# From the third chunk on the first FFN product by Strassen's scheme, with attention pieces at fixed places

## The chip, the cores and the metric

The kernel runs on one core of one Trainium2 chip. The metric is the device time of one execution in microseconds; lower is better. Five engines work side by side, each through its own queue in order: TensorE (PE in the profile; its weight loads are PEld) multiplies, VectorE (DVE) and ScalarE (ACT) do elementwise work and read what TensorE has left in PSUM, GpSimd (POOL) does elementwise work in SBUF, and SyncE (SP) issues the transfers. An instruction that needs another engine's result waits for a semaphore, and everything behind it on its engine waits with it.

## The reference

```python
k_p = k.reshape(B, H, Sp, pool, D).mean(axis=3)      # B = H = 8, S = 576, D = 64, pool = 8, Sp = 72
v_p = v.reshape(B, H, Sp, pool, D).mean(axis=3)
scores = scale * np.matmul(q, k_p.transpose(0, 1, 3, 2))
attn = np.exp(scores - np.max(scores, axis=-1, keepdims=True))
attn = attn / (np.sum(attn, axis=-1, keepdims=True) + 1e-09)
attn_out = np.matmul(attn, v_p)
x = attn_out.transpose(0, 2, 1, 3).reshape(B * S, H * D)      # 4608 tokens x 512
h = x @ w_in                                                  # 512 x 2048
g = np.maximum(h, 0.0) + alpha * np.minimum(h, 0.0)
return (g @ w_out).astype(np.float32)                         # 2048 x 512
```

Keys and values are pooled by eight, each query attends to 72 pooled keys, and the result goes through a feed-forward network (FFN) with a PReLU between its two products.

## The kernel before, in words

The 4608 tokens are cut into nine chunks of 512 (NC = 9, CH = 512). Chunk c has an attention, a first FFN product (w_in, PReLU) and a second one (w_out). A batch entry has 576 tokens, so a chunk spans one or two entries, and all chunks but 0 and 8 bring in one new entry whose K and V are loaded and pooled.

**Precision.** Every fp32 (or wider) operand is split into a high and a low fp16 part, and each product is three matmuls: low by high, high by low, high by high, all added up in PSUM. A weight block of 128x128 is the stationary side.

**FFN.** `ffn1_products(c, f)` (L763) makes the 128 features of block f (16 blocks) for 512 tokens: 4 blocks of K, three matmuls each, 12 matmuls of 512 columns into one PSUM bank of `ps_h`. `ffn1_scaled` (L776, ScalarE), `ffn1_prelu` (L780, VectorE) and `ffn1_parts` (L788 high part on ScalarE, L791 low part on GpSimd) turn it into `g`. `ffn2(c, i)` (L821) makes 128 tokens by 512 outputs: 16 blocks, three matmuls of 512 columns each (L817 to L819), an eviction (L807) and a store (L812). So a chunk has 192 matmuls of 512 columns in each FFN product. The very last tile is made in two halves of 256 columns.

**Attention of a chunk**, per 128-token tile i of four: scores (L602 to L604, 144 columns), maximum L511, subtraction L525, exponential L528 (ScalarE), sum L530, reciprocal L534, scaling L536 (GpSimd), the fp16 parts in `apad` (L545, L548, L551), and a DMA that transposes them into `aT` (L556). Before that K is loaded (`kraw`) and pooled (L376), q is loaded (`qraw`), its maximum taken (L382), the maxima are spread over the partitions (L206 on ScalarE, L209 on TensorE, then L212, L217, L233, L238 on VectorE), and K and q are split (L426, L429, L442, L446). V is loaded (`vraw`), pooled on GpSimd (L467) and split. At the end `mix` (L606, matmuls L613) multiplies by V, and L570 and L574 write x in two fp16 parts.

**Order.** Chunk 0, with the preparation of the weights and the attention of chunks 0 and 1, is ordered by a planner with costs and ranks (`_Plan`, `start`, under a manual schedule). From chunk 1 on the main loop (L924 to L942) writes the code of a chunk, and the attention of the next chunk is dealt out evenly in small groups of operations behind each feature block f, tied by `issue_after` to the last transposition, x and store; the mixes follow the second tile of the second product. A scheduler then orders each engine's queue by its own estimate of when operands are ready, so first and second products, scores and mixes of a chunk stand interleaved on TensorE.

**Buffers.** `big` has 12 buffers of 8 KB per partition; eight of them hold the fp16 weights once they are converted, and kraw, qraw and vraw take turns in the others. `fp` has 4 buffers (pooled K and V, the PReLU tiles, output tiles), `wp` 3 for the exponentials. PSUM: `ps_s` (2 tiles of two banks), `ps_h` and `ps_o` (2 banks each).

## Time and profile before

| what | value |
|---|---|
| runs of the kernel | 872.87, 871.46, 872.85 us; median 872.85 |
| profiled execution: span from the first to the last instruction | 870.4 us (no time of its own besides) |
| granted TensorE clock, mean | 0.994 |
| PE / DVE / ACT / POOL busy | 836.8 / 426.2 / 413.7 / 371.1 us |
| one second product's matmuls plus one first product's | 384 per chunk |
| HBM read / written | 45.10 / 9.44 MB |

Busy times of TensorE come from modelled ends: a matmul's own duration (379 ns for 512 columns) is longer than the step from one to the next, so what a matmul costs is read from the starts in the timeline. A row of a timeline gives start, duration, engine, line, operation, out<-in, shape, count, and in brackets the idle time ahead of it with what ended it. A row of the groups gives the count, then busy time and mean duration, then the idle time ahead with its releasers. SPq rows are SyncE's issues of transfers, not the transfers.

### The profile page before, as it was taken

What the parts mean: (1) busy time and instruction counts of PE and PEld (TensorE: products, weight loads), DVE (VectorE), ACT (ScalarE), POOL (GpSimd) and SP (SyncE); (2) the same over time, 40 slices, a digit from 0 to 9 for tenths busy, and PEclk for the clock granted to TensorE, in tenths of its full rate; (3) what the DMA queues carried; (4) which work ended last, traced back from release to release, by engine and by line L of the source; (5) the groups of instructions that cost most, each with busy time, mean ns of one, the idle gap of its engine ahead of it and who ended that gap; (6) DMA issues with size and microseconds to landing.
All of it is one profiled execution on the core that took longest, in us unless ns stands there. A gap on an engine that the chain in (4) does not pass through costs nothing.

```text
span 870.4 us, 11545 instructions
## 1 busy us (share of the span) xinstructions
PE 836.8 (96%) x4452; PEld 409.4 (47%) x4452; DVE 426.2 (49%) x657; ACT 413.7 (48%) x700; POOL 371.1 (43%) x375
## 2 busy tenths in 40 slices
PE   5769899999999999999999999999999999999998
PEld 4444344445444444454445444544454454444445
DVE  3989998377228621772177207820881156112210
ACT  4989985455425541554145325632562255213330
POOL 1257456187316830683067406731573047203320
PEclk9989999999999999999999999999999999999999
DMA  9686234513710471037003701371126005100000
GB/s 332 229 254 242 78 79 73 180 31 73 209 51 6 83 197 32 20 73 209 26 27 72 210 25 27 66 202 40 28 53 144 17 20 94 37 24 13 1 25 25
DMA packets 122902, 78.87 MB, mean 91 GB/s; under 512 B 106176, under 2 KB 107008, under 8 KB 122848
## 3 DMA queue, kind: packets, MB, share of 16 engines
q1 hardware_dynamic: 122848, 78.14, 33.1%
q8 instruction: 35, 0.57, 0.3%
q14 instruction: 19, 0.16, 0.1%
HBM read 45.10 MB, written 9.44 MB: 63 GB/s over the span
## 4 chain that ended last, share of the span: by engine, by line
PE 85%; DVE 6%; ACT 4%; DMA 3%; issue 1%; SPq 1%; ACTq 0%; DVEq 0%
PE o L817 13%; PE o L819 13%; PE o L818 13%; PE h L770 12%; PE h L771 12%; PE h L772 12%; PE x L613 2%; DMA qraw<-qT_dram 1%; DMA nat<-kN_dram 1%; PE s L602 1%; PE s L603 1%; PE s L604 1%; DVE t L780 1%; PE h L817 1%; PE h L818 1%
## 5 line engine op out<-in xcount | busy, mean ns | idle before, releaser
L791 POOL TENSOR_TENSOR g<-t,g 128x512 f16<-128x512 f32 x144 | 171.9, 1195 | 329.0 <-ACT g L788 327.8
L780 DVE SCALAR_TENSOR_TENSOR t<-t,al 128x512 f32<-128x512 f32 x128 | 128.7, 1007 | 269.1 <-ACT t L776 259.8
L770 PE MATMUL h<-x,w 128*128 128x512 f16 x576 | 218.3, 379 | 4.7 <-DVE w2e L233 1.9
L771 PE MATMUL h<-x,w 128*128 128x512 f16 x576 | 218.3, 379 | 1.1 <-DVE x L574 1.0
L772 PE MATMUL h<-x,w 128*128 128x512 f16 x576 | 218.3, 379 | 0.0
L817 PE MATMUL o<-w,g 128*128 128x512 f16 (+1 forms) x560 | 208.1, 373 | 2.5 <-POOL g L791 1.7
L818 PE MATMUL o<-w,g 128*128 128x512 f16 (+1 forms) x560 | 208.8, 373 | 0.0
L819 PE MATMUL o<-w,g 128*128 128x512 f16 (+1 forms) x560 | 205.6, 373 | 0.0
L788 ACT CAST g<-t 128x512 f16<-128x512 f32 x144 | 88.6, 615 | 115.0 <-DVE t L780 114.5
L776 ACT ACTIVATE t<-h,rp 128x512 f32<-128x512 f32 x144 | 97.9, 681 | 59.6 <-PE h L772 58.9
L807 ACT ACTIVATE o<-o,os 128x512 f32<-128x512 f32 x33 | 22.5, 688 | 165.6 <-PE o L819 165.6
L817 PEld LDWEIGHTS <-g 128*128 128x128 f16 x592 | 57.9, 98 | 69.0 <-POOL g L791 2.7
L467 POOL TENSOR_TENSOR vraw<-vraw 72x512 f32<-72x512 f32 (+1 forms) x56 | 56.6, 1028 | 77.8 <-DMA vraw<-vT_dram 66.8
L819 PEld LDWEIGHTS <-g 128*128 128x128 f16 x592 | 57.9, 98 | 66.5
L771 PEld LDWEIGHTS <-w 128*128 128x128 f16 x576 | 56.3, 98 | 69.0 <-issue 7.1
L818 PEld LDWEIGHTS <-g 128*128 128x128 f16 x592 | 57.9, 98 | 65.5 <-issue 1.3
L772 PEld LDWEIGHTS <-w 128*128 128x128 f16 x576 | 56.3, 98 | 68.7 <-issue 1.6
L770 PEld LDWEIGHTS <-w 128*128 128x128 f16 x576 | 56.3, 98 | 65.0 <-issue 0.6
L574 DVE SCALAR_TENSOR_TENSOR x<-x,xsc,x 128x512 f16<-128x512 f32 x36 | 25.9, 747 | 73.2 <-ACT x L570 73.2
L536 POOL TENSOR_TENSOR e<-e,sm 128x576 f32<-128x576 f32 x35 | 46.2, 1321 | 12.6 <-DVE sm L534 12.2
L548 POOL TENSOR_TENSOR apad<-e,apad 128x448 f16<-128x448 f32 x36 | 40.8, 1134 | 16.0 <-ACT apad L545 16.0
L545 ACT CAST apad<-e 128x576 f16<-128x576 f32 x44 | 28.9, 670 | 24.9 <-POOL e L536 13.9
(137 smaller groups left out, 843.5 us busy)
## 6 DMA issues: line engine op xcount, KB each, us to landing
w<-w_dram SPq DMA_DIRECT2D x16, 1024.0 KB
out_dram<-o SPq DMA_DIRECT2D x35, 256.0 KB
qraw<-qT_dram SPq DMA_DIRECT2D x17, 512.0 KB
vraw<-vT_dram SPq DMA_DIRECT2D x28, 288.0 KB
kraw<-kT_dram SPq DMA_DIRECT2D x12, 576.0 KB
apad<-apad SPq DMA_DIRECT2D x28, 144.0 KB
kq<-kT_dram SPq DMA_DIRECT2D x2, 576.0 KB
nat<-kN_dram SPq DMA_DIRECT2D x2, 512.0 KB
```

What stands on the lines that cost most here:

```text
L467: nc.gpsimd.tensor_tensor(out=o, in0=y, in1=z, op=ALU.add)
L536: x = add("DVE" if i in on_dve else "Pool", us, lambda ex=ex, sm=sm, eng=eng: eng.tensor_tensor(out=ex(), in0=ex(), in1=sm().broadcast_to( ...
L770: nc.tensor.matmul(ps, w[:, 1, ks_], x[:, 0], start=(n == 0), stop=False)
L771: nc.tensor.matmul(ps, w[:, 0, ks_], x[:, 1], start=False, stop=False)
L772: nc.tensor.matmul(ps, w[:, 0, ks_], x[:, 0], start=False, stop=(n == NK - 1))
L776: nc.scalar.activation(t, hps[c, f], AF.Copy, scale=rp[:, f:f + 1])
L780: nc.vector.scalar_tensor_tensor(out=t, in0=t if c else h, scalar=(al if c else ra)[:, f:f + 1], in1=t, op0=ALU.mult, op1=ALU.max)
L788: nc.scalar.copy(out=g[:, 0], in_=t)
L791: nc.gpsimd.tensor_tensor(out=g[:, 1], in0=t, in1=g[:, 0], op=ALU.subtract)
L817: nc.tensor.matmul(ps, g[:, 1, ts_], w[:, 0, cs], start=(f == 0), stop=False)
L818: nc.tensor.matmul(ps, g[:, 0, ts_], w[:, 1, cs], start=False, stop=False)
L819: nc.tensor.matmul(ps, g[:, 0, ts_], w[:, 0, cs], start=False, stop=(f == NF - 1))
```

## The change

From chunk 2 on (`FAST = 2`) the first FFN product is made by the Winograd form of Strassen's scheme, one level deep: features by halves (the even and the odd block of each pair), K by halves and tokens by halves. Seven products of blocks replace eight. For each group d of four feature blocks there are seven `product` calls, each of 12 matmuls (2 pairs q, 2 blocks of K, 3 precision parts) of 256 columns, into three banks x, y and z that are added to more than once:

```diff
+    def product(c, d, bank, n, m, begin, end):
+        if begin:
+            hb[d, bank] = ps_b.tile([P, 2, HC], F32, tag="b", name="h")
+        ps, x = hb[d, bank], xs[c][m]()
+        for q in range(2):
+            for k in range(2):
+                for e, (l, r) in enumerate(((1, 0), (0, 1), (0, 0))):
+                    nc.tensor.matmul(ps[:, q], weights(n, 2 * d + q, l, k), x[:, r, k],
+                                     start=begin and not (q or k or e), stop=end and q + k + e == 4,
+                                     skip_group_check=True)
+    def plus(d, bank, j, n, o=None):
+        z = half(d, j, n)
+        nc.vector.tensor_tensor(out=half(d, *o) if o else z, in0=hb[d, bank], in1=z, op=ALU.add)
+    def fast_begin(c, d):
+        product(c, d, "x", "a11", "b11", True, False)
+        ht[d, 1] = hp_.tile([P, 2, CH], F32, tag="h", name="h1")
+        nc.scalar.copy(out=half(d, 1, 0), in_=hb[d, "x"])
+    def fast_end(c, d):
+        product(c, d, "y", "a22", "t4", False, True)
+        plus(d, "y", 1, 0)
+        product(c, d, "z", "s4", "b22", False, True)
+        plus(d, "z", 0, 1)
+        for j in (1, 0):
+            for q in range(2):
+                f = 4 * d + 2 * q + j
+                hs[c, f] = t = ht[d, j][:, q]
+                nc.scalar.activation(t, t, AF.Copy, scale=rp[:, f:f + 1])
+                nc.vector.scalar_tensor_tensor(out=t, in0=t, scalar=al[:, f:f + 1], in1=t, op0=ALU.mult, op1=ALU.max)
+                ffn1_parts(c, f, 0)
+                ffn1_parts(c, f, 1)
+    def fast_rest(c, d):
+        product(c, d, "y", "s2", "t2", True, False)
+        ht[d, 0] = hp_.tile([P, 2, CH], F32, tag="h", name="h0")
+        plus(d, "y", 1, 0, (0, 1))
+        product(c, d, "z", "s1", "t1", True, False)
+        product(c, d, "x", "a12", "b21", False, True)
+        nc.scalar.copy(out=half(d, 0, 0), in_=hb[d, "x"])
+        product(c, d, "y", "s3", "t3", False, False)
+        plus(d, "y", 1, 0, (1, 1))
+        plus(d, "z", 1, 1)
```

Group d's `fast_begin` is written ahead of `fast_end` of group d - 1 and `fast_rest` of group d. Five `plus` (VectorE) and two copies (ScalarE) per group join the seven products in SBUF tiles h1 and h0. The PReLU part is as before.

The operands: `sums` makes the weight sums s1, s2, s4 (in three `big` buffers that are never given back) and s3 (in place of a block that is no longer used), beside the second product of chunk 1. `blocks` takes the place of L570 and L574 behind the mixes: two evictions of 1024 columns, four differences and seven splits.

```diff
+    def sums(i):
+        a = w16_pair(i)
+        r = hp_.tile([P, 2, CH], F32, tag="h", name="wr")
+        f = hp_.tile([P, 4, HC], F32, tag="h", name="wf")
+        nc.vector.tensor_tensor(out=r, in0=a[:, :, 0], in1=a[:, :, 1], op=ALU.add)
...
+        for n in range(4):
+            nc.scalar.copy(out=outs[n][0], in_=f[:, n])
+            nc.gpsimd.tensor_tensor(out=outs[n][1], in0=f[:, n], in1=outs[n][0], op=ALU.subtract)
+    def blocks(add, c, after, rank):
...
+        for n in range(2):
+            add("PE", 1.1, lambda n=n: mix(c, n, ps[n]()), *after, rank=rank)
+            add("ACT", 1.1, lambda n=n: nc.scalar.activation(f[n](), ps[n](), AF.Copy, scale=xsc), rank=rank)
+        add("DVE", 0.75, lambda: less(srcs["t1"], b[0][1], b[0][0], nc.vector))
+        add("DVE", 0.75, lambda: less(srcs["t2"], b[1][1], srcs["t1"], nc.vector))
+        add("Pool", 1.2, lambda: less(b[0][1], b[1][1], b[0][1], nc.gpsimd))
+        for n, eng in (("b11", nc.vector), ("t2", nc.gpsimd), ("t1", nc.vector), ("b21", nc.vector)):
+            add("ACT", 0.62, lambda n=n: hi(n))
+            add("DVE", 0.75, lambda n=n, eng=eng: lo(n, eng))
+        add("DVE", 0.75, lambda: less(b[1][0], b[1][0], srcs["t2"], nc.vector))
+        for n, eng in (("t3", nc.gpsimd), ("t4", nc.vector), ("b22", nc.gpsimd)):
+            add("ACT", 0.62, lambda n=n: hi(n))
+            add("DVE", 0.75, lambda n=n, eng=eng: lo(n, eng))
```

The attention is cut into eleven stages, and the table `AT` gives each a time within a cycle of 78 us whose first 36.6 are the first product; `on(c, t)` writes the stages of chunks c + 1 and c + 2 that are due. Loads, maxima and scales are now written in the second product of the chunk before last, V and the tiles in the first product of the chunk before, the mix in its second product. The `issue_after` ties go, except around `sums`.

```diff
+AT = dict(load=-19.0, max=-17.0, scale=-10.0, tile0=-4.0, loadv=0.0, v=1.0, tile1=12.0, vscale=20.0, tile2=30.0,
+          tile3=38.0, mix=55.0)
...
+    def on(c, t):
+        for n, at in ((c + 1, t), (c + 2, t - CYCLE)):
+            if n not in lines:
+                lines[n] = _Line(n)
+            lines[n].emit(at)
```

Pools: `ps_h` and `ps_o` become one `ps_b` of four banks, shared by both products. After `start`, `fp` and `wp` are replaced by pools of two buffers each, the second `apad` goes, and `hp_` (four fp32 tiles of 128x1024) and `xq` (three more x tiles) come. The scales `xsc` and `wsc` change by a factor of two each. Chunks 0 and 1 make their products as before.

TensorE's order of chunks 2 to 8 now has the narrow products in groups of 12, with scores, and the first products of the next group, between them; at the end of a first product up to 24 matmuls of the second stand ahead of the last two products of the last group. Of the last 48 matmuls of a second product 27 or 28 stand ahead of the three products that spread the maxima of q and K, and the first scores follow after 22 to 26 narrow matmuls of the next chunk.

SyncE's queue, before: the loads for chunk 5 and the stores of chunk 3 (`aT`: transposition; `kraw`, `qraw`, `vraw`: loads of K, q and V; `out_dram<-o`: stores):

```order
L254 DMA kraw_3943<-kT_dram 128x1152
L254 DMA kraw_3945<-kT_dram 128x1152
L254 DMA qraw_3947<-qT_dram 128x1024 x2
L254 DMA vraw_3950<-vT_dram 72x1024 x2
L812 DMA out_dram<-o_3714 128x512
L812 DMA out_dram<-o_3766 128x512
```

The same place in the changed kernel:

```order
L568 DMA_TRANSPOSE aT_3550<-apad0_96 128x16x128
L948 DMA out_dram<-o_4208 128x512
L259 DMA kraw_4345<-kT_dram 128x1152
L948 DMA out_dram<-o_4324 128x512
L259 DMA qraw_4347<-qT_dram 128x1024 x2
L948 DMA out_dram<-o_4395 128x512
L948 DMA out_dram<-o_4506 128x512
L259 DMA vraw_4524<-vT_dram 72x1024 x2
L259 DMA vraw_4527<-vT_dram 72x1024 x2
```

The two halves of K, q and V went out in a row ahead of the stores; now the second half of K, q and V stand between and behind the stores (the first half, kraw_4343, stands eight rows further up).

VectorE's queue in the first product of chunk 4, before (pt, pr, ev, vs: scale of V; mx, e, sm: softmax of a tile; t: PReLU; os: output scale; v16: low part of V):

```order
L212 TENSOR_REDUCE pt_4106<-pm_4104 128x1
L217 TENSOR_SCALAR pr_4108<-pt_4106 128x1
L233 TENSOR_SCALAR ev5_4110<-pr_4108 128x1
L511 TENSOR_REDUCE mx_4153<-s_4138 128x8
L238 TENSOR_SCALAR vs__4131<-ev5_4110 128x1
L801 TENSOR_TENSOR os_5401<-wsc_120,ev5_4110 64x1
L801 TENSOR_TENSOR os_5456<-wsc_120,ev5_4110 128x1
L525 TENSOR_TENSOR e_4155<-s_4138,mx_4153 128x576
L487 SCALAR_TENSOR_TENSOR v16_4133<-vs_4069,vs__4131,v16_4133 72x512
L780 SCALAR_TENSOR_TENSOR t_4171<-t_4171,al_116 128x512
```

The same place now (h1 is the SBUF sum, h_4659 bank y and h_4674 bank z of the second group; vm: the maximum of the pooled V):

```order
L914 SCALAR_TENSOR_TENSOR h0_4543<-h0_4543,al_116 128x512 x2
L247 TENSOR_REDUCE vm_4803<-vs_4587 72x1
L897 TENSOR_TENSOR h1_4611<-h_4659,h1_4611 128x2x256
L523 TENSOR_REDUCE mx_4727<-s_4714 128x8
L897 TENSOR_TENSOR h1_4611<-h_4674,h1_4611 128x2x256
L537 TENSOR_TENSOR e_4729<-s_4714,mx_4727 128x576
L217 TENSOR_REDUCE pt_4810<-pm_4808 128x1
L222 TENSOR_SCALAR pr_4812<-pt_4810 128x1
L238 TENSOR_SCALAR ev5_4814<-pr_4812 128x1
L243 TENSOR_SCALAR vs__4816<-ev5_4814 128x1
```

The additions of the banks (L897) stand among the steps of V and of the softmax, where before there were PReLUs.

More of the change, by code (lines that the diff above doesn't have):

```diff
@@ L302, in big_tile, with attention @@
         return once(lambda: big.tile(shape, F32, tag="big", name=name))
-    def attention(add, c, bs, rank, begin=False, early=False, k_pool=0, q_cuts=1, on_act=(), on_dve=(), behind=()):
+    def attention(add, c, bs, rank, begin=False, early=False, k_pool=0, q_cuts=1, on_act=(), on_dve=(), behind=(), stage=lambda n: None):
+        stage("load")
         n = len(bs) + 2
@@ L384, in attention @@
             ld, rank=rank + 0.18 * i) for i, (q, (t, ld)) in enumerate(zip(q16s[c], ql))]
+        stage("scale")
         scs = []
@@ L499, in attention @@
         for i in range(TPC):
+            stage(f"tile{i}")
             rk = rank + rks["sm"] + rks["sms"] * i
@@ L561, in attention @@
         xd = []
+        stage("mix")
+        if c >= FAST:
+            blocks(add, c, [*td, *vd], rank)
+            return xd, td
         for hp in range(NPR // 2):
```

143 lines of the change are left out of this document (103 added, 40 removed).

## The prediction

> **What bounds the kernel now.** I read the page first, then the chain of work that ended last, the busy time by stretches, the groups of instructions by shape, and the timelines. The page:
>
> ```profile
> span 870.4 us, 11545 instructions
> PE 836.8 (96%) x4452; PEld 409.4 (47%) x4452; DVE 426.2 (49%) x657; ACT 413.7 (48%) x700; POOL 371.1 (43%) x375
> PE 85%; DVE 6%; ACT 4%; DMA 3%; issue 1%; SPq 1%; ACTq 0%; DVEq 0%
> ```
>
> TensorE is busy 96% of the span and carries 85% of the chain. The stretches (length, then busy time of PE, PEld, DVE, ACT, POOL) show where the rest lies:
>
> ```profile
> 160.00:180.00 20.00, 18.89 (x90) 8.69 (x90) 8.00 (x13) 11.09 (x20) 7.16 (x6) 1.00 0.70 223
> 180.00:200.00 20.00, 18.12 (x109) 9.08 (x108) 18.41 (x30) 11.01 (x17) 15.82 (x18) 1.00 0.02 5
> 231.00:320.00 89.00, 89.00 (x482) 42.71 (x481) 42.51 (x64) 37.92 (x61) 40.78 (x41) 1.00 0.39 97
> 408.00:497.00 89.00, 89.00 (x481) 42.72 (x480) 42.00 (x64) 37.75 (x61) 41.04 (x40) 1.00 0.32 83
> 488.00:508.00 20.00, 20.00 (x117) 9.64 (x116) 2.91 (x4) 7.20 (x13) 3.64 (x4) 1.00 0.54 178
> ```
>
> Chunk 1 begins at about 161 us and loses 1.1 + 1.9 us there; in the later stretches TensorE has no gap, at granted clock 1.00 (the column behind POOL), and the other engines have half their time free. So a microsecond taken from TensorE in chunks 2 to 8 is a microsecond of the kernel, as long as the others keep up. The mixes (attention times V) in the chain mark the period:
>
> ```profile
> 229.04 1.91 PE x L613 x32
> 317.91 1.90 PE x L613 x32
> 406.02 1.90 PE x L613 x32
> ```
>
> The period is 88.1 to 88.9 us. The prices of a matmul come from TensorE's timeline, as first and last start of gapless runs:
>
> ```profile
> 254.63 0.38 PE L772 MATMUL h<-x,w 128*128 128x512 f16 x1
> ...
> 256.57 0.38 PE L772 MATMUL h<-x,w 128*128 128x512 f16 x1
> ...
> 276.65 0.23 PE L602 MATMUL s<-kbd,q 128*128 128x144 f16 x1
> ...
> 277.34 0.23 PE L604 MATMUL s<-kbd,q 128*128 128x144 f16 x1
> ...
> 863.04 0.27 PE L819 MATMUL o<-w,g 128*128 128x256 f16 x1
> ...
> 866.97 0.27 PE L819 MATMUL o<-w,g 128*128 128x256 f16 x1
> ```
>
> Nine steps of 512 columns take 1.94 us (0.2156 each), eleven of 144 columns 0.69 (0.063), 36 of 256 columns 3.93 (0.1092). All load new weights each time; a load is hidden even behind 144 columns.
>
> **The gain.** A first FFN product of a chunk is 192 matmuls of 512 columns, 41.4 us. By seven block products it is 4 x 7 x 12 = 336 of 256 columns, 36.7 us. That is 4.7 us less in each of chunks 2 to 8: 32.9 us, all of it on the path.
>
> The Trainium skill speaks against this: "TensorE: Matmul & The Clock Gate", section "Back-to-back issue gap", gives a stream of load-and-matmul pairs about 81 ns at 128 columns and 131 at 512. By these two figures half the columns keep three quarters of the spacing, and the scheme would lose. The rows above deny it here: 0.1092 is 51% of 0.2156.
>
> **What the change puts on the other engines.** The prices, from the groups of instructions (count | busy us, mean ns of one | idle time before and its releasers):
>
> ```profile
> L780 DVE SCALAR_TENSOR_TENSOR t<-t,al 128x512 f32<-128x512 f32 x128 | 128.7, 1007 | 269.1 <-ACT t L776 259.8 <-issue 5.2 <-POOL apad L551 4.0
> L780 DVE SCALAR_TENSOR_TENSOR t<-h,m,t 128x512 f32<-128x512 f32 x16 | 11.8, 747 | 1.1 <-ACT t L776 1.1
> L776 ACT ACTIVATE t<-h,rp 128x512 f32<-128x512 f32 x144 | 97.9, 681 | 59.6 <-PE h L772 58.9 <-ACT t L776 0.5
> L788 ACT CAST g<-t 128x512 f16<-128x512 f32 x144 | 88.6, 615 | 115.0 <-DVE t L780 114.5
> L791 POOL TENSOR_TENSOR g<-t,g 128x512 f16<-128x512 f32 x144 | 171.9, 1195 | 329.0 <-ACT g L788 327.8 <-PE h L772 1.3
> L511 DVE TENSOR_REDUCE mx<-s 128x8 f32<-128x576 f32 x36 | 26.5, 737 | 5.6 <-PE s L604 5.5
> L382 ACT ACTIVATE q<-qraw 128x1024 f16<-128x1024 f32 x17 | 17.8, 1048 | 7.6 <-DMA qraw<-qT_dram 7.6
> L664 DVE SCALAR_TENSOR_TENSOR vw<-vw,w 128x1024 int32<-128x1024 int32 x14 | 17.1, 1224 | 1.2 <-ACT vw L661 1.2
> L530 DVE TENSOR_REDUCE sm<-e 128x8 f32<-128x576 f32 x32 | 23.9, 748 | 17.2 <-ACT e L528 17.2
> L532 DVE TENSOR_SCALAR sm<-sm 128x8 f32<-128x8 f32 x36 | 11.6, 323 | 0.9 <-ACT e L521 0.4
> L206 ACT ACTIVATE pd<-ident,m 128x128 bf16<-128x128 bf16 x42 | 14.6, 395 | 3.1 <-DVE m L242 2.1 <-PE pm L209 0.8
> L242 DVE TENSOR_REDUCE vm<-vs 72x1 f32<-72x512 f32 x8 | 5.4, 673 | 0.0
> L242 DVE TENSOR_REDUCE m<-ks 128x1 f32<-128x288 f32 x8 | 3.6, 447 | 0.8 <-ACT ks L297 0.8
> ```
>
> *Sums of weights*, once, beside chunk 1's second product: 8 times one 128x1024 (L664's 1.22) and four 128x256 operations (nearest row 0.45) on VectorE, 24 us, less on ScalarE, about the same on GpSimd. 41.4 us of TensorE work hide it, in a stage where VectorE is busy 2.9 of 20 us. Uncovered it would cost up to 24; I take 0.
>
> *Blocks of x*, behind each mix: seven high parts and two evictions on ScalarE (7 x 0.615 + 2 x 1.05 = 6.4 us), seven operations on VectorE (7.0 at 1.007), four on GpSimd (4.8 at 1.195). They stand against 22 us of products that follow: 0. The moved scale factors cost nothing.
>
> *First FFN product.* Per group of four feature blocks VectorE gets five additions that read PSUM (`plus`), ScalarE two copies; a product into a bank must wait until the addition before it has read that bank. The tightest place: after `s3`x`t3` into bank y comes `a22`x`t4` into the same bank, with one or two other products (1.3 to 2.6 us) between. VectorE's order at such a place is quoted with the change.
>
> Behind `vm`, which waits for GpSimd's pooling of V, stand two additions for which TensorE waits; before, only PReLUs stood there. VectorE's sum in the stage: 20 additions at 0.75 (14.9), 16 PReLUs at 1.007 (16.1), four tiles of three softmax passes at 0.74 (8.9) and of two small ones at 0.32 or less (2.2), V 2.5 (its maximum 0.67, its low part like a PReLU, five small ones), q 1.24: 45.8 us, against 36.7 + 3.4 of scores = 40.1 on TensorE. Records overlap a little (the rows below: 0.75 long, the next starts 0.67 later), 70 long ones by 0.08, so 40.3 is the true load: equal to TensorE's, with the last tile's part running into the second product. Waits are then between 0 and 45.8 - 40.1 = 5.7 us per stage, in six stages (chunk 8 has no attention beside it: 31 us).
>
> ```profile
> 432.16 0.75 DVE L780 SCALAR_TENSOR_TENSOR t<-t,al 128x512 f32<-128x512 f32 x1 [19.94 <-ACT t L776]
> 432.83 2.60 DVE L376 TENSOR_REDUCE ks<-kraw 128x144 f32<-128x1152 f32 x2
> ```
>
> I take 0.5 a stage, 3 us, nearest to 40.3. I price `plus` by L780's PSUM form (747). The Trainium skill ("SBUF — State Buffer", "Who interferes with whom") says that a VectorE operation with two SBUF inputs contends with a GpSimd one that reads SBUF, and one with a single SBUF input doesn't; by it 747 holds, and if `plus` took 1007 too the sum would be 51.0. The two rows agree with the page, which no run here tries on `plus` itself.
>
> *Loads.* Three of the 12 `big` buffers go to the weight sums for good and eight hold weights, so one is left for K, q and V: each load waits until the one before is used up. SyncE's queue is quoted with the change. K and q once went out together ahead of the stores; now q waits for the second half of K, and that for the reduction of the first, which VectorE does behind the first block of x. The rows, from the timelines of SyncE, VectorE and ScalarE (idle time and releaser in brackets; chunk 1, and chunk 4 from 442 us on):
>
> ```profile
> 163.19 1.34 SPq L254 DMA_DIRECT2D kraw<-kT_dram  x2
> 164.63 0.94 SPq L254 DMA_DIRECT2D qraw<-qT_dram  x2
> ...
> 167.78 1.35 DVE L376 TENSOR_REDUCE ks<-kraw 128x144 f32<-128x1152 f32 x1 [2.36 <-DMA kraw<-kT_dram]
> ...
> 172.10 1.06 ACT L382 ACTIVATE q<-qraw 128x1024 f16<-128x1024 f32 x1 [1.06 <-DMA qraw<-qT_dram]
> ...
> 174.76 1.06 ACT L382 ACTIVATE q<-qraw 128x1024 f16<-128x1024 f32 x1 [1.01 <-DMA qraw<-qT_dram]
> ...
> 442.68 0.55 DVE L212 TENSOR_REDUCE pt<-pm 128x3 f32<-128x384 f32 x1
> ...
> 448.95 2.48 DVE L446 SCALAR_TENSOR_TENSOR q<-qraw,s,q 128x1024 f16<-128x1024 f32 x2
> ```
>
> From the mix to the first scores: eviction 1.05, subtraction 0.75, reduction 1.35, K load 4.6 (163.19 to 167.78), reduction 1.35, q load 7.5 to 10.1 (164.63 to 172.10 or 174.76), maximum 1.05, its spread over partitions 3 x 0.395 and a product, 2.5 in all, pt to the first half of q 7.5 (442.68 to 450.2, PReLUs between): 26.6 to 29.2 us. In TensorE's order lie 102 wide and 22 narrow products between, 24.4 us. The wait is 2.2 to 4.8 us a chunk; without PReLUs, stores and V in the way it is 0. I take 0.8 in each of six chunks, 5 us, near the low end: this order puts scores, mixes and maxima just behind their operands as the old one did, and TensorE shows no gap in the two long stretches quoted.
>
> *Chunk 1*: the `f` buffers fall from 4 to 2, shared with K and V. While K or V holds one, an f takes 0.68 + 1.01 + 0.62 + 1.20 = 3.5 us instead of 2.6, 0.9 for each of up to eight: 7 us at worst. q is loaded earlier, and the 3 us lost now can go: -3 at best. I take +1.
>
> **The sum.** 870.4 - 32.9 + 3 + 5 + 1 = 846.5 us of span. The profiled execution is known by its span; the three runs lie at 871.46 to 872.87, the median 872.85, 2.4 above it. So 849.
>
> **Rivals.**
> - *No waits at all.* The gapless stretches of before speak for it, engines at 90 to 100% in the first product against it: 870.4 - 32.9 + 2.4 = 840.
> - *The single load buffer is the bound.* At 2.5 us in six chunks, 15 instead of 5: 859; at 4.8 it is 29: 873, no gain. For it: the rows of chunk 1; against: there 1 MB of stores and V stood in the same queue.
> - *VectorE is the bound of the first product* (slower). Place: the additions into banks y and z. Price: 5.7 us in six stages, 34.2 instead of 3: 846.5 + 31.2 + 2.4 = 880. It decides from 44.8 us of VectorE time per stage on, where the 4.7 gained are gone. For it: 45.8 by mean durations, PReLUs of up to 2.7 us; against: the overlap of records, and the last group's additions wait beside second products.
> - *The weight loads set the pace of narrow matmuls* (slower). Place: every product of 256 columns. If a load (98 ns by the row below) no longer hid wholly and each step were that and the shortest one seen, 0.063, it would be 0.161: 336 x 0.161 = 54.1, 12.7 us more in seven chunks instead of 4.7 less: 970. For it: the loads grow from 192 to 336; against: the 36 steps of 0.1092. The two figures of the Trainium skill's page would have it so.
>
> ```profile
> L817 PEld LDWEIGHTS <-g 128*128 128x128 f16 x592 | 57.9, 98 | 69.0 <-POOL g L791 2.7 <-issue 1.5
> ```
>
> **How the numbers follow.** Forecast (843 to 856) 0.59; no waits 0.16; load buffer 0.15 (of which 0.02 at no gain); VectorE 0.09; weight loads 0.01. A measurement here can tell 0.2%, 1.7 us. Faster 0.59 + 0.16 + 0.13 = 0.88; same 0.02; slower 0.10. The range is 839 to 862: no waits, forecast, and most of the load case; left out are the slower ones and the worst loads, 0.15 or so.
>
> **What would show it.** Right: 336 products per chunk stepping at 0.109 us, the period near 85 us, PE gaps short and in front of the scores (released by VectorE's q) and of `a22`x`t4` (released by `plus`). The load case: gaps of over 2 us at the maxima's product or the first scores, with ScalarE's maximum waiting for the q load. The VectorE case: `plus` starting late with no idle time ahead of it, and PE waiting for it in every group. Wrong altogether: a step well above 0.11, or more than 5 us of gaps per chunk.

## The result, and the profile after

The changed kernel takes 897.86 us (median of 4 runs, 897.56 to 899.88), the kernel before 872.86: 1.028 times as long, 95% interval 1.0255 to 1.031. Two executions, one of the run e1 below (2487.6 us) and the profiled one of e5 (983.8 us at a granted clock of 0.82), were far slower than the others of their kernel and are left out of all times. The profiled execution has a span of 895.8 us, 25.4 more than before. The head of its page:

```profile
span 895.8 us, 13939 instructions
PE 820.9 (92%) x5460; PEld 514.4 (57%) x5460; DVE 572.0 (64%) x858; ACT 472.8 (53%) x823; POOL 442.8 (49%) x435
PE 36%; DVE 16%; DMA 10%; POOL 10%; issue 5%; ACT 3%; POOLq 0%; SPq 0%; ACTq 0%; DVEq 0%
```

TensorE carried 85% of the chain that ended last and now carries 36%; VectorE, DMA and GpSimd have taken the rest. TensorE's busy time fell by 15.9 us where 32.9 were forecast, and its idle time grew by 895.8 - 820.9 - (870.4 - 836.8) = 41.3 where 9 were. These two differences, 17.0 and 32.3, are the whole miss of 49.3 us.

Where it happened: the stretches from mix to mix (length, then busy time of PE, PEld, DVE, ACT, POOL, then the granted clock), chunk 1's part, chunk 2, and the next three.

```profile
160.00:240.00 80.00, 69.22 (x343) 31.98 (x343) 46.49 (x76) 35.62 (x60) 43.64 (x45) 0.96 0.28 63
240.00:351.00 111.00, 91.93 (x629) 59.70 (x628) 90.18 (x114) 53.42 (x99) 70.45 (x70) 0.90 0.28 68
351.00:441.00 90.00, 86.39 (x599) 57.73 (x598) 59.09 (x84) 45.78 (x74) 47.06 (x45) 0.95 0.35 79
441.00:532.00 91.00, 86.56 (x633) 57.45 (x633) 55.58 (x86) 45.11 (x74) 47.27 (x44) 1.00 0.36 83
532.00:619.00 87.00, 84.44 (x618) 56.72 (x619) 56.42 (x84) 44.53 (x74) 46.76 (x44) 1.00 0.35 84
```

Before, every period from chunk 2 on was 88 to 89 us, and chunk 1's was 74. Now chunk 2 takes 111 with VectorE busy 90 of them, chunks 3 and 4 about 90, and only then does the period come down to 87, where it stays until chunk 7 (85). The granted clock is below 1.00 in the first three stretches, where before it was 1.00 from chunk 1 on. The longest waits of TensorE from chunk 1 on, from its timeline (idle time and releaser in brackets):

```profile
181.49 0.24 PE L675 MATMUL s<-kbd,q 128*128 128x144 f16 x1 [4.43 <-DVE q L455]
216.10 0.38 PE L847 MATMUL h<-x,w 128*128 128x512 f16 x1 [2.14 <-ACT t L853]
270.50 0.26 PE L214 MATMUL pm<-pd,ones 128*128 128x128 bf16 x1 [6.97 <-ACT pd L211]
301.32 2.94 PE L887 MATMUL h<-x,w 128*128 128x256 f16 x15 [2.84 <-ACT h L902]
310.07 2.72 PE L887 MATMUL h<-x,w 128*128 128x256 f16 x12 [5.82 <-DVE h L897]
351.18 2.99 PE L686 MATMUL x<-aT,v 88*64 88x320 f16 x24 [3.62 <-DMA aT<-apad]
410.00 0.27 PE L887 MATMUL h<-x,w 128*128 128x256 f16 x1 [2.17 <-DVE h L897]
531.93 1.70 PE L686 MATMUL x<-aT,v 88*64 88x192 f16 x27 [2.33 <-DMA aT<-apad]
```

The 6.97 us have a history that VectorE's timeline tells:

```profile
228.18 0.91 DVE L857 SCALAR_TENSOR_TENSOR t<-t,al 128x512 f32<-128x512 f32 x1 [1.77 <-ACT t L853]
229.01 1.21 DVE L642 TENSOR_TENSOR wr<-w 128x1024 f32<-128x1024 f16 x1
...
251.72 1.34 DVE L384 TENSOR_REDUCE ks<-kraw 128x144 f32<-128x1152 f32 x1
...
261.17 1.34 DVE L384 TENSOR_REDUCE ks<-kraw 128x144 f32<-128x1152 f32 x1
...
272.15 0.78 DVE L646 TENSOR_TENSOR wf<-wr,wf 128x256 f32<-128x256 f32 x1
272.85 0.54 DVE L217 TENSOR_REDUCE pt<-pm 128x3 f32<-128x384 f32 x1
```

The weight sums are pinned behind chunk 1's last PReLU, which ends at 229; they last until 273, through the blocks of x and into chunk 2's first product. The first K reduction of chunk 3 stands behind four of the eight sums, the beginning of a fifth and the first operations of the blocks of x until 251.7, the second behind more of both until 261.2, and SyncE's and ScalarE's rows hang on it, because there is one load buffer:

```profile
253.08 0.34 SPq L259 DMA_DIRECT2D kraw<-kT_dram  x1
262.54 0.81 SPq L259 DMA_DIRECT2D qraw<-qT_dram  x2
...
266.14 1.06 ACT L390 ACTIVATE q<-qraw 128x1024 f16<-128x1024 f32 x1 [1.64 <-DMA qraw<-qT_dram]
```

Each load is issued as soon as the reduction before it is over. So the sums, priced at nothing, arrive at TensorE by way of the load chain: the late reductions and the one buffer work together.

### The profile page after: what moved, and what is told of

Same layout as the page of the kernel before. It is cut to its first block, busy times and chain, and to the rows that moved or that the text cites. A ratio compares the mean times of both kernels' runs of the same rounds, so it can differ in the third digit from the quotient of the medians.

```text
span 895.8 us, 13939 instructions
## 1 busy us (share of the span) xinstructions
PE 820.9 (92%) x5460; PEld 514.4 (57%) x5460; DVE 572.0 (64%) x858; ACT 472.8 (53%) x823; POOL 442.8 (49%) x435
## 4 chain that ended last, share of the span: by engine, by line
PE 36%; DVE 16%; DMA 10%; POOL 10%; issue 5%; ACT 3%; POOLq 0%; SPq 0%; ACTq 0%; DVEq 0%
PE h L887 10%; PE o L953 8%; PE o L955 8%; PE o L954 8%; DMA aT<-apad 5%; DMA vraw<-vT_dram 4%; POOL vraw L477 3%; DVE h L914 3%; POOL g L868 3%; DVE h L897 2%; DVE wf L646 2%; POOL e L548 1%; PE x L686 1%; DMA apad<-apad 1%; DVE sm L542 1%
## 5 line engine op out<-in xcount | busy, mean ns | idle before, releaser
L887 PE MATMUL h<-x,w 128*128 128x256 f16 x1344 | 166.2, 277 | 13.6 <-DVE h L897 9.7
L868 POOL TENSOR_TENSOR g<-h,g 128x512 f16<-128x512 f32 x112 | 136.5, 1245 | 82.8 <-ACT g L865 82.8
L897 DVE TENSOR_TENSOR h<-h,h 128x512 f32<-128x512 f32 x140 | 94.3, 683 | 70.7 <-PE h L887 60.5
L887 PE MATMUL h<-x,sw 128*128 128x256 f16 x1008 | 126.1, 276 | 0.1
L914 DVE SCALAR_TENSOR_TENSOR h<-h,al 128x512 f32<-128x512 f32 x112 | 112.3, 1055 | 0.8 <-ACT h L913 0.8
L887 PEld LDWEIGHTS <-sw 128*128 128x128 f16 x1008 | 99.3, 99 | 13.3 <-issue 0.2
L913 ACT ACTIVATE h<-h,rp 128x512 f32<-128x512 f32 x112 | 73.9, 713 | 47.3 <-DVE h L897 46.5
L865 ACT CAST g<-h 128x512 f16<-128x512 f32 x112 | 64.5, 616 | 19.8 <-DVE h L914 19.4
L560 POOL TENSOR_TENSOR apad<-e,apad 128x448 f16<-128x448 f32 x36 | 40.1, 1113 | 37.1 <-ACT apad L557 37.1
L847 PE MATMUL h<-x,w 128*128 128x512 f16 x128 | 49.7, 388 | 5.4 <-ACT t L853 3.9
L868 POOL TENSOR_TENSOR g<-t,g 128x512 f16<-128x512 f32 x32 | 37.6, 1182 | 30.2 <-ACT g L865 30.2
L848 PE MATMUL h<-x,w 128*128 128x512 f16 x128 | 49.6, 388 | 1.1 <-DVE x L590 1.0
```

The costliest lines, as they stand in the source:

```text
L847: nc.tensor.matmul(ps, w[:, 1, ks_], x[:, 0], start=(n == 0), stop=False)
L865: last["h"] = nc.scalar.copy(out=g[:, 0], in_=t)
L868: last["g"] = nc.gpsimd.tensor_tensor(out=g[:, 1], in0=t, in1=g[:, 0], op=ALU.subtract)
L887: nc.tensor.matmul(ps[:, q], weights(n, 2 * d + q, l, k), x[:, r, k], start=begin and not (q or k or e), stop=end and q + k + e == 4, skip ...
L897: nc.vector.tensor_tensor(out=half(d, *o) if o else z, in0=hb[d, bank], in1=z, op=ALU.add)
L913: nc.scalar.activation(t, t, AF.Copy, scale=rp[:, f:f + 1])
```

## The experiments

Times are medians, ratios those to the kernel before, measured beside each run, with their 95% interval. Runs are called by their number.

**e1, e2, e3, e4: one suspect each.**

e1 makes no sums and has

```diff
-FAST = 2
+FAST = NC
...
+            for t in sw:
+                nc.vector.memset(t[:, 0, 0, :4], 1.0)
...
+        if c == NC - 2:
+            for t in sw:
+                nc.vector.tensor_scalar(out=t[:, 0, 0, :4], in0=t[:, 0, 0, :4], scalar1=2.0, scalar2=None, op0=ALU.mult)
```

The two small operations were to hold the three buffers `sw` until the end. They do not: the scheduler puts both into chunk 1, at 170 us, and the loads take the buffers from there on. The rows are those of e2, which has the same lines; e5, e7 and e11 have them too, and show the same:

```profile
170.07 0.17 DVE L1112 TENSOR_SCALAR sw<-sw 128x4 f16<-128x4 f16 x1
170.27 8.51 SPq L259 DMA_DIRECT2D kraw<-kT_dram  x2
```

Both halves of K, q and V of chunk 3 go out by 184 us; K is reduced at 246. So e1, e2, e5, e7 and e11 have four load buffers, as the kernel before has, where their expectations speak of three held ones or a single one.

> No product by Strassen's scheme in any chunk; the fixed places of the attention pieces, the smaller pools and the three buffers held for the weight sums stay as in the changed kernel. Before 872.9, changed 897.9. Theory A (three separate losses: chunk 1's two buffers for f, the weight sums, and VectorE with the late transpositions in chunks 2 to 7): only the first and a part of the last remain, chunk 1 about 10 us longer, late transpositions up to 8: 880 to 890. Rival C (the new places and the load buffer cost most of it, whatever the product): 890 or more. Rival B (VectorE's additions and PReLUs alone): within 4 us of before.

Measured: 910.8 us, 1.043 (1.038 to 1.048), in rival C's range, though without its load buffer. The order and the pools alone, even with the loads' buffers given back, are slower than with Strassen's scheme. TensorE's waits name the cause:

```profile
PE h L847 <- ACT t L853: 20.4, 11, 3.3
```

The evictions into f, which now has two buffers, hold the first product up in chunks 1 to 5. In the changed kernel chunk 1 is the only one of these that isn't done by the scheme. e7 and e11 take this apart.

e2 leaves the sums out, with e1's lines on `sw`:

```diff
-        if n in ("s1", "s2", "s4"):
-            return sw[("s1", "s2", "s4").index(n)][:, i, l, cs]
-        j, h = dict(a11=(0, 0), a12=(0, 1), a22=(1, 1), s3=(1, 0))[n]
+        j, h = dict(a11=(0, 0), a12=(0, 1), a22=(1, 1), s3=(1, 0), s1=(0, 0), s2=(0, 1), s4=(1, 1))[n]
...
-                if c == FAST - 1 and f % 8 == 0:
+                if False:
```

> The sums of weights are left out: the products by Strassen's scheme take blocks of the old weights in their place (the numbers are wrong, the number and size of matmuls is the same), the three buffers stay held. Theory A: chunk 2's period of 111 us falls to about 90, the whole by 15 to 22 us, to 876 to 883. Rival B (the first product is bound by VectorE whatever ran before): chunk 2 keeps most of its loss, 892 or more.

Measured: 859.7 us, 0.985 (0.980 to 0.989), 38.2 us less than the changed kernel: twice what even the first theory gave. The gain isn't in chunk 2 alone. Stretches of e2, from chunk 2's mix on:

```profile
245.00:329.00 84.00, 82.14 (x589) 55.07 (x588) 57.93 (x86) 43.62 (x73) 51.28 (x45) 1.00 0.35 84
329.00:413.00 84.00, 83.81 (x615) 56.29 (x612) 54.16 (x84) 44.21 (x74) 49.50 (x45) 1.00 0.34 87
```

Without the sums, and with four load buffers, the scheme gives what was forecast of it: from chunk 3 on periods of 84 to 85 us, hardly a gap, clock 1.00, with nearly the same VectorE time as in the changed kernel's later chunks (54 to 58 us a chunk). So VectorE's time does not bind by itself. But two things were changed here, since the buffers came free with the sums: how much of the 38.2 us each is worth, and what the single buffer would cost without the sums, no run shows.

e3 gives chunk 1 other f buffers:

```diff
-        hs[c, f] = t = fp.tile([P, CH], F32, tag="f", name="t")
+        hs[c, f] = t = (hp_ if c else fp).tile([P, CH], F32, tag="h" if c else "f", name="t")
```

> Chunk 1's sixteen f tiles come out of the four buffers of the other pool, which nothing uses in that stage; K and V keep the two. Theory A: the period of chunk 1 falls from 84.6 towards the 73.9 of before, 6 to 10 us less: 888 to 892. Rival (the gaps of chunk 1 come from the late q load and from the order, not from the f buffers): 895 or more.

Measured: 882.8 us, 1.010 (1.006 to 1.014): 15.1 less, half again as much as the most that the first theory said. In this run TensorE stands still for 11.4 us ahead of chunk 2's mix (at 240.83), and the profile names nothing that it waited for.

e4 leaves one line out of `fast_end` (L914):

```diff
-                nc.vector.scalar_tensor_tensor(out=t, in0=t, scalar=al[:, f:f + 1], in1=t, op0=ALU.mult, op1=ALU.max)
```

> In chunks 2 to 8 the PReLU is left out (16 VectorE operations of 1.06 us less per chunk; ScalarE and GpSimd take the scaled tile at once). Theory A: the waits for additions and copies in the first products go (about 11 us of gaps with 3 to 5 of half clock behind them), the rest stays: 882 to 888. Rival B (VectorE is the bound of the whole loss): below 877.

Measured: 874.7 us, 1.002 (0.999 to 1.004): 23.2 less, in the range of the rival. VectorE's time does decide here. Since e2 has all PReLUs and hardly a gap, it decides together with the sums and the one buffer, where VectorE is already late.

**e5 and e7: do they add up, and what does the order cost?** e5 is e2 and e3 together; e7 is e1 with the f buffers of e3.

> Both edits at once: chunk 1's f tiles out of the other pool, and the sums of weights left out (blocks of the old weights in their place, wrong numbers, the same matmuls). If the sums and chunk 1's two buffers, with all that they make late, are the whole of the miss, what is left is the forecast's sum without these two: 845 to 851. If VectorE or the single load buffer binds by itself, chunks 2 to 7 stay above 86 us a period and the time above 856.

> The run without any Strassen product again, now with f tiles out of four buffers in every chunk. That run lost 39 us against before, with TensorE waiting for ScalarE's evictions into f twice a chunk. If those two buffers are its loss, 870 to 877; if the fixed places or the one load buffer cost by themselves, 885 or more.

Measured: e5 854.8 us (three executions), 0.979 (0.975 to 0.983), only some 5 less than e2, and between its two ranges. The two edits overlap: without the sums and with four load buffers, chunk 1's buffers for f cost little. e7 888.4 us, 1.018 (1.013 to 1.022): above the range for the first case and inside that of the second; with four load buffers, this leaves the places. The f buffers were 22 us of e1's loss, and some 14 remain. TensorE's waits in e7:

```profile
PE x L686 <- DMA aT<-apad: 11.4, 5, 4.8
```

The mix waits for the last transposition in chunk after chunk: the new places put the last tiles too late.

**e8 and e9: loads in halves, done badly.** The single 8 KB load buffer was to become two halves, but K's last third was written ahead of the reduction of the first third, whose place it takes; one third of K is not used, and the order of the waits is not that of two buffers. (e9 also has e3 and four early sums.)

> The changed kernel with the one buffer for K, q and V loads used as two halves in turn (K in thirds, q and V each in pieces that fill a half); sums and chunk 1 as they were. Load theory (the sums make the loads late once, and a single buffer keeps them late in every later chunk): chunks 1 and 2 as before, the periods of chunks 3 to 7 from 88 on average to 84 or 85, 880 to 886. VectorE theory (its work in the first product makes the later waits): 893 or more.

> The three mended together, with all of the work done: f tiles of chunk 1 out of the other pool, halved load buffer, and four of the eight weight sums moved into chunk 1's first product (behind its 6th, 9th, 12th and 15th feature block), the rest into the first half of its second product. If sums, f buffers and loads are the cause, each chunk loses a microsecond or so of waits: 848 to 858. If the sums still cost where they stand now, 860 to 870.

Measured: 905.2 us (1.036, 1.033 to 1.040) and 899.4 (1.029, 1.026 to 1.033), far above their first ranges. They decide nothing on loads. One row of e8 on ScalarE is worth having, though:

```profile
399.04 1.06 ACT L406 ACTIVATE q<-ld 128x1024 f16<-128x1024 f32 x1 [4.09 <-DMA ld<-qT_dram]
...
400.10 0.76 ACT L556 ACTIVATE e<-e,ds 128x576 f32<-128x576 f32 x1
```

An operand that is 4 us late holds the exponential behind it, VectorE's row sum waits for that, and TensorE then waited 4.57 us for the addition behind the row sum. An attention piece that stands too early in an engine's queue can cost as much as one that stands too late.

**e10 to e13: the loads again, the places, the sums' place.** e10 is the edit that e8 was meant to be: the next load is written behind the reduction that empties its half.

```diff
-            step = NPR * S // 2
+            step = NPR * S // (3 if c >= 3 else 2)
...
+                if c >= 3 and a == 2 * step:
+                    later.append(go)
...
+                    if later:
+                        later.pop(0)()
...
+            ld_[:] = [big.tile([P, 2, 1024], F32, tag="big", name="ld"), 0]
```

> The edit that the run of halved loads was meant to be: the one buffer for K, q and V as two halves in turn (K in thirds), now with each later load written behind the reduction or pooling that empties its half, so that nothing is overwritten. Sums and chunk 1 as in the changed kernel. TensorE's order from chunk 3 on is then nearly that of the run without sums (maxima's products 16 us of work behind the mix, for 20.5). Load theory (the sums make the loads late once, a single buffer keeps them late): periods of chunks 3 to 7 fall from 88 to about 85, 880 to 888. If the loads are not what makes the later waits: 893 or more.

Measured: 881.8 us, 1.010 (1.008 to 1.013), 16.1 less, inside the load theory's range. Its stretches, chunk 2 to chunk 4:

```profile
240.00:344.00 104.00, 90.04 (x618) 58.42 (x617) 77.85 (x114) 52.90 (x98) 69.71 (x70) 0.93 0.30 70
344.00:429.00 85.00, 84.39 (x617) 56.33 (x617) 52.85 (x85) 44.88 (x74) 46.28 (x45) 1.00 0.37 86
429.00:517.00 88.00, 85.22 (x626) 57.00 (x626) 55.47 (x87) 45.30 (x74) 47.14 (x44) 1.00 0.31 79
```

Chunk 3 is free of loss at once. A second buffer lets the loads catch up after the sums; with a single one chunks 3 and 4 still take about 90 us, and VectorE, with little to spare, turns late loads into waits. From chunk 4 on (88 us here) the two kernels are within 3 us of each other in every period.

e11 moves the tiles in e7:

```diff
-AT = dict(... tile1=12.0, vscale=20.0, tile2=30.0, tile3=38.0, mix=55.0)
+AT = dict(... tile1=8.0, vscale=20.0, tile2=20.0, tile3=30.0, mix=55.0)
```

> The run without Strassen and with four f buffers (888 against 874 for before), whose only gaps are five waits of the mix for the last transposition, 1.0 to 4.8 us, 11.4 in all: now the tiles' places are moved up (second to fourth tile at 8, 20 and 30 for 12, 30 and 38), which puts the last scores 5 us of TensorE's work further ahead of the mix. If the fixed places make the transposition late: 874 to 880, the waits gone. If the single padded buffer does it, whatever the place: 885 or more.

Measured: 877.3 us, 1.005 (1.003 to 1.0065), and no wait of a mix for the transposition is left. It was the place and not the single padded buffer (`apad`). What the order then still costs without the scheme, and with four load buffers, is about 4 us; the largest wait left is one of 6.0 us for GpSimd at chunk 1's second product.

e12 is e3 with four of the eight sums in chunk 1's first product and four in the first half of its second:

```diff
                 on(c, HALF * f / NF)
+                if f in {5: 0, 8: 1, 11: 2, 14: 3}:
+                    with tc.issue_after(last["p"].ins), tc.issue_after(last["h"].ins), tc.issue_after(last["g"].ins):
+                        sums({5: 0, 8: 1, 11: 2, 14: 3}[f])
...
-                if c == FAST - 1 and f % 8 == 0:
+                if c == FAST - 1 and (i, f) in {(0, 0): 4, (0, 8): 5, (1, 0): 6, (1, 8): 7}:
...
```

> f tiles of chunk 1 out of the other pool (882.8 alone), and half of the weight sums moved up into chunk 1's first product (behind its 6th, 9th, 12th and 15th feature block), the rest into the first half of the second. If it is their place behind the first product that makes chunk 2 late, 868 to 876; if it is their work on VectorE and GpSimd wherever it stands, 880 or more.

Measured: 876.8 us, 1.005 (1.002 to 1.007): 6.0 less than e3, a little above the first range. The place counts; the run stays 4 us above the kernel before.

e13 has all of these (without e11's places) and the operands of the sums in PSUM:

```diff
-        r = hp_.tile([P, 2, CH], F32, tag="h", name="wr")
+        r = ps_s.tile([P, 2, CH], F32, tag="s", name="wr")
...
-        nc.vector.tensor_tensor(out=r, in0=a[:, :, 0], in1=a[:, :, 1], op=ALU.add)
-        a11, a12, a21, a22 = (r[:, j, n * HC:n * HC + HC] for j in range(2) for n in range(2))
+        nc.vector.tensor_tensor(out=r[:, 0], in0=a[:, 0, 0], in1=a[:, 0, 1], op=ALU.add)
+        nc.vector.tensor_tensor(out=r[:, 1, HC:], in0=a[:, 1, 0, HC:], in1=a[:, 1, 1, HC:], op=ALU.add)
+        nc.vector.tensor_tensor(out=f[:, 3], in0=a[:, 1, 0, :HC], in1=a[:, 1, 1, :HC], op=ALU.add)
+        a11, a12, a21, a22 = r[:, 0, :HC], r[:, 0, HC:], f[:, 3], r[:, 1, HC:]
```

> All of it with the work done in full: f tiles of chunk 1, half of the sums early, two half buffers for the loads, and three of the four blocks of each weight sum held in PSUM, so that three of the four additions read one SBUF operand. By the rows of the changed kernel an addition of the sums takes 0.41 us alone and 0.89 beside GpSimd: VectorE's part falls from 33 us towards 25. If sums, f buffers and loads are the loss: 855 to 865. If the sums cost wherever they stand: 872 or more.

Measured: 872.4 us, 1.000 (0.998 to 1.002): the time of before, on the other theory's side. With sums in chunk 1's first product, where VectorE has other work, the waits go there.

**e14 to e17: contention, and another chunk for the sums.** e14 is the changed kernel with the PSUM edit above and nothing else.

> The changed kernel (897.9) with one edit: of each weight sum, a11, a12 and a22 are held in PSUM instead of SBUF, so that three of its four additions read one SBUF operand. Contention theory: those additions take 0.41 for 0.89 us, VectorE's part falls by about 10 us, GpSimd's subtractions from 1.0 to 0.8, and chunk 2 starts its attention earlier: 885 to 892. If the sums cost by their place alone: 895 or more.

Measured: 884.5 us, 1.013 (1.011 to 1.016), 13.4 less, just below its first range. The groups of the sums' additions and of GpSimd's subtractions behind them, changed kernel:

```profile
L646 DVE TENSOR_TENSOR wf<-wf,wr 128x256 f32<-128x256 f32 x8 | 6.6, 828 | 0.0
L646 DVE TENSOR_TENSOR wf<-wr,wf 128x256 f32<-128x256 f32 x8 | 5.9, 740 | 0.1
L650 POOL TENSOR_TENSOR sw<-wf,sw 128x256 f16<-128x256 f32 x24 | 23.6, 997 | 7.4 <-ACT sw L649 7.3
```

and e14:

```profile
L648 DVE TENSOR_TENSOR wf<-wf,wr 128x256 f32<-128x256 f32 x16 | 6.6, 410 | 0.2
L648 DVE TENSOR_TENSOR wf<-wr,wf 128x256 f32<-128x256 f32 x16 | 6.0, 414 | 0.1
L652 POOL TENSOR_TENSOR sw<-wf,sw 128x256 f16<-128x256 f32 x24 | 17.2, 741 | 8.4 <-ACT sw L651 8.4
```

The same addition takes about half the time when one operand is in PSUM, and GpSimd's part falls by a quarter: with two operands in SBUF the two engines stood in each other's way. The Trainium skill ("SBUF — State Buffer", section "SBUF: two separate sides") says just that: a VectorE operation with two SBUF inputs and a GpSimd one that reads SBUF share a port pair, and one waits for the other. The groups agree: in the changed kernel, too, the same addition takes 0.41 us where GpSimd pauses (at 262.44 and 267.00).

The 13.4 us are not the price of this contention alone, though. The first additions of each sum, one of 1024 columns before (10.8 us in all), are three now and take 7.4 + 5.7 + 4.9 = 18.0, so that VectorE's part falls only from 33.4 to 30.6 us and not by the 10 that were expected. And the order of VectorE's queue came out differently: the sums begin at 221, and the first K reduction of chunk 3 starts at 237.9, with half of the sums still behind it, where it started at 251.7.

e15, e16 and e17 set `FAST = 3` on e13's edits: e15 with four sums in each product of chunk 2, e16 with two and six, e17 as e15 with e11's places.

> The scheme begins one chunk later (six chunks by it), with f tiles from the other pool, two half buffers, sums in PSUM, four of them in the first product of the last ordinary chunk and four in its second. Against the same edits from the third chunk on (872.4): the gain falls by 4.7. Clash theory (the sums cost so much because chunk 1 still carries the start's late attention): its 15 to 20 us of loss in chunks 1 and 2 become 5 to 8: 858 to 866. If the sums cost that much anywhere: 873 or more.

> As the run before, but two sums in the first product (behind its 10th and 14th feature block) and six in the first half of the second, where VectorE is idle in an ordinary chunk. Clash theory: 857 to 866, within 3 us of the run before. If sums beside the second product hold up the next attention as they did: 868 or more.

> As e15 with the tiles' places at 8, 20 and 30, which took 11 us of late transpositions off the run without the scheme. If the late transposition is a cost here too: 3 to 6 us below e15. If VectorE's queue is what makes it late, the same as e15 or more.

Measured: e15 883.4 us (1.012, 1.009 to 1.014), e16 871.6 (0.998, 0.996 to 1.000), e17 871.4 (0.997, 0.996 to 0.999). The clash with chunk 1 is not the cause: e13 and e15, with the same edits, differ by 11 us, of which one chunk less by the scheme is 4.7, so beside an ordinary chunk the sums cost no less. e16 lies in its second range. It also gives 11.8 us against e15 for moving two of the sums to the second product. Moving the tiles up gave 12 us in e17 against e15, twice the most that was expected.

**e18 and e19: all that was found, together.** e18 has from the third chunk on e3's f buffers, e10's half buffers, the sums in PSUM at their first place, and e11's places. e19 starts the scheme a chunk later and spreads the sums over two chunks.

> From the third chunk on as in the changed kernel, work done in full: f tiles from the other pool, two half buffers, sums in PSUM at their first place (second product of chunk 1), tiles' places at 8, 20 and 30. The four losses found so far taken away together, the sums not in the way of chunk 1's first product (e13: 872.4, with them there). If the losses add up: 856 to 864. If the sums hold up chunk 2's attention by their work alone: 868 or more.

> The scheme from the fourth chunk on, the sums spread thinly: three of the four blocks of sums 0 to 3 beside chunk 1's second product, the rest beside chunk 2's; f tiles, half buffers and PSUM as before, the tiles' places as in the changed kernel. If it is the sums' density beside one chunk that costs (period 95 to 99 against 88 in the three runs before), 860 to 867; if their work delays the next attention wherever it stands, 870 or more.

Measured: e18 865.2 us, 0.990 (0.987 to 0.994): 1% faster than the kernel before, with all of the work done, 32.6 us below the changed one and 8.9 below before; a little outside its first range. e19 877.8, 1.004 (1.003 to 1.006), in its second range: this spreading does not help. It makes some of the blocks of four sums twice, so it is not a clean test of their density. One row of e18's stretches shows what is left:

```profile
230.00:327.00 97.00, 87.07 (x632) 57.67 (x634) 73.61 (x117) 51.46 (x95) 63.62 (x70) 0.98 0.31 78
```

Chunk 2 still takes 97 us, 10 more than the 87 of e2 (from 242.71 to 329.43).

**The runs side by side**, in us from chunk 1's first mix to chunk 3's, and from there to the end of the span, by the profiled executions (those of e4 and e14 are 4 us below their medians); the second line is the first with nothing but the forecast's gain taken off (one period in the first column, six in the second):

| run | chunks 1 and 2 | chunk 3 to the end |
|---|---|---|
| before (155.06, 317.84, 870.4) | 162.8 | 552.6 |
| before less 4.7 a chunk | 158.1 | 524.4 |
| changed | 195.9 | 544.6 |
| e2, no sums, four load buffers | 174.0 | 528.2 |
| e3, f buffers | 182.5 | 543.2 |
| e4, no PReLU | 178.8 | 534.2 |
| e10, two half buffers | 189.7 | 535.9 |
| e14, sums in PSUM | 184.5 | 539.7 |
| e18, all | 170.9 | 537.3 |

The rows that mark it: most of chunk 3's mix in the changed kernel stands at 351.18, quoted above, and the whole of it in e2 and e18 here:

```profile
329.43 1.97 PE L686 MATMUL x<-aT,v 88*64 88x192 f16 x32
```

```profile
326.63 1.97 PE L730 MATMUL x<-aT,v 88*64 88x192 f16 x32
```

In the changed kernel 8 of the 32 products of this mix stand earlier (from 341.65 on), and five more products of the second FFN product stand ahead of 351.18 than ahead of 329.43 in e2. That is 1.6 us of work, so the columns are good to 2 us.

## Why the prediction was wrong, point by point

*The gain (32.9 us): right.* A group of twelve still starts every 1.31 us where nothing is in the way, 0.1092 a step:

```profile
740.73 1.47 PE L887 MATMUL h<-x,w 128*128 128x256 f16 x12
742.04 1.47 PE L887 MATMUL h<-x,sw 128*128 128x256 f16 x12
```

The weight-load rival is refuted, and e2's chunks 3 to 8, with four load buffers, take 528.2 us where the gain alone gives 524.4.

*Sums of weights (0): the step that failed.* It said that 41.4 us of TensorE work hide 24 us of VectorE in a stage where VectorE is busy 2.9 of 20 us. The other groups of the sums in the changed kernel, and, in the kernel before, the whole stretch of chunk 1's second product:

```profile
L642 DVE TENSOR_TENSOR wr<-w 128x1024 f32<-128x1024 f16 x8 | 10.8, 1347 | 0.0
L646 DVE TENSOR_TENSOR wf<-wr 128x256 f32<-128x256 f32 x16 | 10.1, 668 | 0.2
```

```profile
203.00:245.00 42.00, 42.00 (x228) 19.77 (x226) 14.71 (x22) 18.58 (x31) 20.96 (x21) 1.00 0.61 151
```

Three things were wrong. With the two groups that stand at e14, VectorE's part is 10.8 + 10.1 + 6.6 + 5.9 = 33.4 us, not 24: the 0.45 was the price of a reduction with one operand, and 0.67 to 0.83 were measured for the additions with GpSimd beside them. VectorE's other work in this stage is 14.7 us, and 14.7 + 33.4 = 48 do not fit into 42; the 2.9 of 20 were read in a part of another chunk's stage. And the sums start at 229, pinned behind the last PReLU, when the x blocks and two K reductions with a load chain behind them are about to come. The rows above show what came of it: a wait of 6.97 us and the half clock behind it in chunk 2. The cost is not 0: half of the sums elsewhere gave 6.0 us (e12 against e3), another form of them 13.4 (e14). Its size stays open. Leaving the sums out was worth 38.2, more than the "up to 24" of the forecast, but with three buffers given back to the loads. Of these 38.2, some 20 to 22 us lie in chunks 1 and 2 and 16 to 18 behind them (table: 195.9 - 174.0 and 544.6 - 528.2), where the sums are long over.

*Blocks of x (0): not refuted.* In e2, with them behind every mix, there is hardly a gap.

*Single load buffer (5): the chain was right, the term too small.* Two half buffers gave back 16.1 us. That the rival on record has 15 us, 2.5 in each of six chunks, is luck: the waits at the maxima's product behind chunk 2's mix are these,

```profile
PE pm L214 <- ACT pd L211: 10.8, 5, 7.0
```

6.97 us once, 1.26 and 1.58 in the next two chunks, and 0.47 in each of two more. The buffer passes on a delay that something else made. The forecast took the chain from the mix to the first scores without the sums in it. Whether the buffer would cost anything without them is open, because every run without the sums had four.

*VectorE's additions (3): too small as well, under the same conditions.* The forecast had 45.8 us of VectorE in the stage by mean durations, called 40.3 the true load, and named 44.8 as the point from which it decides. The 40.3 takes an overlap off 70 long operations, while its own list has 51; with these it is 41.7, above TensorE's 40.1. The price of `plus` held: its 140 additions take 0.64 to 0.69 us each, also while GpSimd works. Taking 112 PReLUs away gave 23.2 us; in e2, with them, there is hardly a gap left to take. In chunk 2's first product three PReLUs in a row took 7.07 us, 2.4 each, while GpSimd worked:

```profile
296.33 4.35 DVE L544 TENSOR_SCALAR sm<-sm 128x8 f32<-128x8 f32 x1
300.59 1.72 DVE L914 SCALAR_TENSOR_TENSOR h<-h,al 128x512 f32<-128x512 f32 x1
...
302.35 7.07 DVE L914 SCALAR_TENSOR_TENSOR h<-h,al 128x512 f32<-128x512 f32 x3
309.34 0.68 DVE L897 TENSOR_TENSOR h<-h,h 128x512 f32<-128x512 f32 x1
```

The addition at the end is the one that TensorE waited 5.82 us for. The rival on record, "VectorE is the bound" at 880, came nearest to the measured time, but as a cause it was no more than a part.

*Chunk 1 (+1): wrong in size.* Even in e2 chunks 1 and 2 take 174.0 us for 158.1. Other f buffers alone gave 15.1 us back with the sums in place and some 5 without them (e5), where 7 were put down as the worst case. That worst case counted the longer stay of each f, and not the q split and the scores that wait for it (4.43 us at 181.49, a wait that e3 does not have), nor the sums that then start later.

*Not in the forecast: the places and the clock.* The places of the last tiles make the transposition late (waits of 3.62 and 2.33 us in the changed kernel and two shorter ones; e7 and e11 show the cause). And waits cost more than their length, since the clock falls behind some of them (below): up to 13.6 of the 17.0 us that TensorE's busy time is over the forecast.

*What stays open.* The edits of e2, e3, e10, e14 and e4 give back 38, 15, 16, 13 and 23 us, 105 for a miss of 49: they cut the same chain at several points, so no share can be given to each. The sums and the single buffer were not parted: a run without the sums and with one load buffer is missing. Why e18 still takes 10 us more than e2 in chunk 2 and 9 more behind it was not taken apart. Nor was the clock tried by itself; what it costs is worked out from the rows.

## What to carry to other kernels

Work "hidden beside" a stage has to be checked against the operations that stand behind it in the same in-order queue: who waits for the K reduction, the row sum, the addition there, and what is loaded when they are done. A bound on such a cost is not the work's own length: where a load chain runs through a single buffer, a delay made once can be paid again in the chunks behind it (16 us went with a second buffer, e10). A run that leaves something out can also free more than it names: here the buffers came back with the sums, which the loads' issue times show. And a change that brings in a faster scheme together with smaller pools and a new order should be costed, and tried, as three changes: here the scheme gave its 33 us, and the rest took 58.

## What the runs showed of the hardware that was not expected

Short gaps can lower TensorE's clock. Stretches of 4 us (length, PE's busy time, then the granted clock) behind the gaps that end at 216.10 and at 531.93 in the changed kernel:

```profile
216.00:220.00 4.00, 3.90 (x11) 0.57 0.64 120
...
532.00:536.00 4.00, 4.00 (x39) 1.00 0.00 0
```

From chunk 1 on the granted clock is 0.50 in six stretches of this kernel, from 182.3, 216.5, 267.7, 301.8, 349.6 and 411.0 us on. Their sum (length, then busy times):

```profile
sum 37.54, PE 27.26 PEld 16.59 DVE 25.33 ACT 17.72 POOL 21.84; mean PE 4.54 PEld 2.76 DVE 4.22 ACT 2.95 POOL 3.64
```

Behind a gap of 2.14 us the clock falls to half, behind one of 2.33 it doesn't, and twelve narrow products behind the 5.82 us gap take 2.72 us in place of 1.47 (row at 310.07 above). TensorE is busy in 27.3 of the 37.5 us at half clock, so that the clock costs at most 13.6 us; 17.0 are missing from the busy time, and the rest is not accounted for. The Trainium skill ("TensorE: Matmul & The Clock Gate", section "Part 1: The HAM clock gate") has the array fall to half its clock after an idle window of about 3.4 us, and the windows run freely; here gaps of 2.1 us were enough, and one of 2.3 was not.

VectorE's small operation at 296.33, 128x8 and 0.32 us on average before, took 4.35 while GpSimd worked without a pause. The two-operand rule as given above does not cover it, since it reads one tile; what held it was not tried. The mean of this operation rose from 323 to 479 ns:

```profile
L544 DVE TENSOR_SCALAR sm<-sm 128x8 f32<-128x8 f32 x36 | 17.2, 479 | 0.7 <-ACT e L533 0.4
```
